# Seven down products in the first half of a SwiGLU block, with sums on preloaded PSUM banks and weight remainders split during attention

## The chip, the cores and the metric

The kernel runs on one core of a Trainium2 chip. The metric is the device time of one execution in microseconds (us); lower is better. The engines are named as in the profile: PE is TensorE (matmuls; PEld its weight loads), DVE is VectorE, ACT is ScalarE, POOL is GpSimd, SP is SyncE, which here issues DMAs.

## The reference

One transformer block over 2048 tokens of width 576, all in float32: a layer norm modulated by a condition vector, an attention with 32 heads of 18 in four segments of 512 tokens with a linear memory carried from segment to segment, then a second modulated norm and a SwiGLU feed-forward network of width 4608.

```python
h = _layernorm(x) * (1 + ca) + sa
x = x + ga * _A_ref(h, A_wq, A_wk, A_wv, A_wo, A_beta)   # attention, 4 segments, memory M, z
h = _layernorm(x) * (1 + cb) + sb
x = x + gb * ((_silu(h @ w_gate) * (h @ w_up)) @ w_down) # 576 -> 4608 -> 576
```

## The kernel before

The block runs in three stages: projections (to about 270 us), attention (to about 610 us), and the feed-forward network. Float32 matmuls are done by splitting an operand into a rounded high part (`fp32r`) and a low remainder (original minus high part), and adding three products: high x high, high x low, low x high. So each operand costs a cast on ScalarE (`wh`, `ah`, `dh`) and a subtraction on VectorE (`wl`, `al`, `dl`).

**Attention.** 32 units u (segment, group of four heads), each of 11 steps k. Per unit, TensorE makes the scores of one unit twice: once for the row maxima (L182, reduced by VectorE at L187), once shifted by the maxima (L599); ScalarE takes the exponentials into `Pt` (L602), GpSimd masks the diagonal (L606), TensorE multiplies by V (`av`, L619). Work of other kinds is put at fixed steps by the table `PAT`, or by `at(g, f)`, which runs f at step g = 11 u + k.

**Feed-forward.** Tokens are taken in two halves t of 1024, the hidden width in 18 passes p of 256 (`NPR`). Gate and up products are made with Strassen's scheme in Winograd's form: per pass and per z (0 gate, 1 up) seven products m of 2 x 2 blocks instead of eight, so a pass has 14 steps k, in the order `ZM`. A product is seven matmuls of 512 columns (`prod`, L1200): six on two blocks of 128 rows in their three split parts, and one on the 32 remaining rows of each 288-row block. For that one, tile `R[z]` (`wr`) holds the remaining rows three times over: high part, low part, high part. The weights of a pass lie in tile `O[p, z]`: slots 0, 1, 2, 3 are loaded, slots 3 to 6 end as sums (`sum_o`, GpSimd); the remaining rows are stored beside them, four times over, as a third group of 128 columns. In the first half `prep_r` casts the high parts into `R[z]` (ScalarE, L1149), `later` subtracts the low parts (VectorE, L1150), and `store_r` writes `R[z]` to memory (`rD`). In the second half `prep_r` loads `R[z]` from there, and `load_o` loads the sums that `store_o` stored.

The banks A (two), B and C take the products. ScalarE copies one product into bank B before the next is added to it (L1246), so sums of products are made in PSUM. `fin` takes Silu and gate times up, into `AC[i, j]`, the four blocks of the activation.

**Down projection.** The activation of pass p is multiplied by `w_down` during pass p + 1, chunk by chunk, between the products. `is_plain(t, p)` decides how: all of the first half, and the last two passes of the second half, are plain. A plain pass has eight chunks of 2 x 6 matmuls of 288 columns, four activation blocks (`prep_a`) and four weight blocks (`prep_d`), and each chunk is added by VectorE to its accumulator (L1325). A pass that is not plain has seven products of two chunks each, of 2 x 3 matmuls; it needs sums of activation blocks (`sum_a`, VectorE, L1271), seven `prep_a` and seven `prep_d`, and its fourteen chunks are added by VectorE to eight accumulators `acc[0..7]` (L1309), which are combined at the end (`comb`). The weights of a pass lie in the one tile `RW[p]`: loaded (`load_d`), multiplied by the output gate (`mul_d`, GpSimd), summed (`sum_d`, GpSimd), and stored for the second half (`wdD`). Plain chunks run at the steps set in `CH0[t]`, the others at those in `CH` (two at steps 4 and 11, none at 6 and 13).

All chunks use two PSUM tiles of two banks each, in turn (tag `dn`). The first half also makes the second half's operands (`prep2`: norm of the last tokens, transposes into a `dn` tile, splits on ScalarE and VectorE, sums on GpSimd, stores by SyncE), step by step in passes 1 to 16.

Every engine works through its instructions in the order in which the program lists them. The order within a step k is: weight casts for five products ahead (`prep_w`, `PF` = 5), subtractions left over from the step before (`later`), Silu that waited (`acts`), the product, loads, sums, the chunk, `prep_d`, `prep_a`.

The lines of the code that a sentence can't say are these; `POS` gives the product of chunks 2i and 2i + 1:

```python
CH = (1, 1, 1, 1, 2, 1, 0, 1, 1, 1, 1, 2, 1, 0)
ZM = [(z if m != 3 else 1 - z, m) for z in range(2) for m in (1, 3, 6, 2, 7, 5, 4)]
POS = [1, 4, 2, 5, 6, 7, 3]
```

Of the kernel before, what the change touches and what calls it, by code (L numbers as in the profile page):

```python
# [15 lines left out]
P = 128  # L16
# [21 lines left out]
CH0 = ((0, 0, 0, 0, 1, 1, 1, 1, 1, 1, 1, 1, 0, 0), (0, 0, 0, 1, 1, 1, 1, 1, 1, 1, 1, 0, 0, 0))  # L38
RS = {(0, 5): 2, (0, 6): 4, (0, 8): 3, (0, 10): 5, (1, 9): 2, (1, 11): 3, (1, 13): 4}
# [24 lines left out]
LNA = 1  # L64
S1B, S2B, XB, WB = 2, 2, 2, 1
# [7 lines left out]
def block(ctx: ExitStack, tc: tile.TileContext, x, wqk, wv, wo, beta, wgu, wd, c, w_mod, out):  # L73
# [76 lines left out]
    rD = [[dr.tile([96, 7, P], F32, tag=f"rD{p}_{z}", name=f"rD{p}_{z}") for z in range(2)] for p in range(NF // 2)]  # L150
# [898 lines left out]

    def prep2(x2p):  # L1050
# [4 lines left out]
        def opr(kb, hv, o, f):  # L1055
            n = P if kb < 2 else 96
            st = x2p.tile([P, 2, 256], F32R, tag="st", name="st", bufs=4)
# [28 lines left out]
        for kb in range(3):  # L1086
            n = P if kb < 2 else 96
            for hv in range(2):
                for kh in range(2):
# [10 lines left out]
                    pt = ps.tile([P, 2, L], F32, tag="dn", name="pt", bufs=2)[:, 0].rearrange("p (a b) -> p a b", b=P)  # L1100
# [31 lines left out]
    def load_o(t, p, z):  # L1132
        O[p, z] = o = opl.tile([P, 7, 3, P], F32, tag="O", name="O", bufs=2)
        if t == 0:
            nc.sync.dma_start(o[:, 0:4], wgu[p, z])
        else:
            nc.sync.dma_start(o[:, 0:3, 0:2], wgu[p, z][:, 0:3, 0:2])
            nc.sync.dma_start(o[:, 3:7, 0:2], oD[p][z])

    def store_o(p, z):  # L1140
        nc.scalar.dma_start(oD[p][z], O[p, z][:, 3:7, 0:2])

    def prep_r(t, p, z, part=0):
        r = R[z]
        if t == 1:
            (nc.sync if p or z == 0 else nc.scalar).dma_start(f32(r[0:96]), rD[p][z])
            return
        o, c = O[p, z], slice(0, 3) if part == 0 else slice(3, 7)
        nc.scalar.copy(r[0:96, c], o[0:96, c, 2, :])  # L1149
        later.append(lambda: nc.vector.tensor_tensor(r[32:64, c], o[32:64, c, 2, :], f32(r[32:64, c]), op=ALU.subtract))  # L1150

    def sum_o(p, z, j, eng=nc.gpsimd):
        o = O[p, z]
        d, a, b, op = ((4, 3, 2, ALU.add), (5, 4, 0, ALU.subtract), (3, 0, 3, ALU.subtract), (6, 1, 5, ALU.subtract))[j]
        eng.tensor_tensor(o[:, d], o[:, a], o[:, b], op=op)  # L1155

    def store_r(p, z):
        nc.scalar.dma_start(rD[p][z], f32(R[z][0:96]))

    def prep_w(p, z, m):  # L1160
        o = O[p, z][:, SLOT[m], 0:2]
# [123 lines left out]

    def load_x11(t):
# [9 lines left out]
    def down(t, p, c):  # L1296
        m, c = POS[c // 2], c % 2
        ah, al = AP[p % 2, m]
        dh, dl = DP[p % 2, m]
        pd = ps.tile([P, 2, L], F32, tag="dn", name="pd", bufs=2)  # L1300
        for i in range(2):
            tk = slice(128 * (2 * c + i), 128 * (2 * c + i) + 128)
            for k, (a, w) in enumerate(((ah, dh), (ah, dl), (al, dh))):
                nc.tensor.matmul(pd[:, i, :288], lhsT=a[:, tk], rhs=w, start=(k == 0), stop=(k == 2))  # L1304
        o = acc[m][:, 2 * c:2 * c + 2]
# [5 lines left out]
    def plain(t, p, c):  # L1311
        b, h, c = c // 4, c // 2 % 2, c % 2
        pd = ps.tile([P, 2, L], F32, tag="dn", name="pd", bufs=2)
# [9 lines left out]
        d = x11[1] if t and b and h else acc[2 + h + 2 * b]  # L1323
# [8 lines left out]
    def comb(j):  # L1332
        d, b = ((2, 1), (0, 5), (6, 1), (5, 6), (3, 5), (7, 6), (4, 7), (0, 7))[j]
        d = acc[d] if d else x11[1]
        nc.vector.tensor_tensor(d, d, acc[b], op=ALU.add)

    def is_plain(t, p):
        return t == 0 or p >= NPR - 2

    with tc.manual_schedule():  # L1340
# [5 lines left out]
        for u in range(NU + 1):  # L1346
# [4 lines left out]
            for k in range(11):  # L1351
                next(ga, None)
                next(gb, None)
                if u == 17 and k == 0:
# [30 lines left out]
        load_o(0, 0, 1)  # L1385
        load_y(0, 1)
# [13 lines left out]
        for i in range(4):  # L1400
            for h in range(2):
                for c in range(WC):
# [12 lines left out]
                    if n in WW:  # L1415
                        j = WW.index(n)
                        if j < 2:
                            prep_r(0, 0, 0, j)
# [26 lines left out]
        for t in range(2):  # L1445
            for p in range(NPR):
                last = t == 1 and p == NPR - 1
# [3 lines left out]
                if t == 0 and p == 1:  # L1451
                    p7.close()
                    x2p = pool(p6, "x2p")
                    g2 = prep2(x2p)
                if t == 0 and p == NPR - 1:
                    run(g2)
                    p6.close()
                    accq = pool(p4, "acq")
                    new_acc(accq, (1, 6, 7))
                if last:  # L1460
                    load_x11(1)
                chunk = 0
                for k in range(14):
# [6 lines left out]
                    for f in todo:  # L1470
                        f()
                    while acts:
# [14 lines left out]
                    if t:  # L1487
                        if k == 2 + swap:
                            prep_r(1, p, 1)
                        elif not last and k == 9:  # L1490
                            prep_r(1, nx, 0)
                    else:
                        if k in (3, 5):
                            prep_r(0, p, 1, k // 5)
                        elif tn == 0 and k in (9, 10):
                            prep_r(0, nx, 0, k - 9)
                        elif tn and k == 8:
                            prep_r(1, 0, 0)
# [16 lines left out]
                        if not dl and k in (6, 7, 8, 9) and p < NPR - 2:  # L1515
                            sum_d(p, k - 6)
# [3 lines left out]
                        elif k == 3:  # L1520
                            store_r(p, 0)
                        elif k == 8:
# [112 lines left out]
```

## Time and profile before

| | us |
|---|---|
| median of 3 runs | 1904.1 (1901.33 to 1904.87) |
| profiled execution | 1902.24 |
| its span, first to last instruction | 1900.5 |
| granted TensorE clock, mean | 0.996 |

The profile is of one execution. A busy time is the time in which an engine had at least one instruction under way; group rows add up the durations of their instructions, which can overlap a little. Waits are given as "who <- whom: us in total, times, longest". The chain of waits is followed back from the last instruction of the program: at each step to what released it.

The page's view of forty equal slices shows the three stages in GpSimd's line and in the DMA's:

```profile
PE   6999999999999899999999999999999999999999
DVE  6566358878886688898898888876888888888887
ACT  1222267768767444445454454444445454454542
POOL 5212236555556555545544545400000000000000
```

Each digit is the busy share of 47.5 us in tenths; the first half of the feed-forward network is the part in which GpSimd works after the thirteenth slice, the second half the part in which it rests.

### The profile page before, as it was taken

What the parts mean: (1) busy time and instruction counts of PE and PEld (TensorE: products, weight loads), DVE (VectorE), ACT (ScalarE), POOL (GpSimd) and SP (SyncE); (2) the same over time, 40 slices, a digit from 0 to 9 for tenths busy, and PEclk for the clock granted to TensorE, in tenths of its full rate; (3) what the DMA queues carried; (4) which work ended last, traced back from release to release, by engine and by line L of the source; (5) the groups of instructions that cost most, each with busy time, mean ns of one, the idle gap of its engine ahead of it and who ended that gap; (6) DMA issues with size and microseconds to landing.
All of it is one profiled execution on the core that took longest, in us unless ns stands there. A gap on an engine that the chain in (4) does not pass through costs nothing.

```text
span 1900.5 us, 30716 instructions
## 1 busy us (share of the span) xinstructions
PE 1862.9 (98%) x10927; PEld 1559.2 (82%) x10927; DVE 1509.0 (79%) x3277; ACT 933.8 (49%) x2060; POOL 584.4 (31%) x789
## 2 busy tenths in 40 slices
PE   6999999999999899999999999999999999999999
PEld 4888866676766788888888888888888888888888
DVE  6566358878886688898898888876888888888887
ACT  1222267768767444445454454444445454454542
POOL 5212236555556555545544545400000000000000
PEclk9999999999999899999999999999999999999999
DMA  6767555446654854454454454378343233333331
GB/s 190 259 221 249 200 193 155 132 136 175 184 159 127 282 201 160 157 196 158 153 189 158 164 171 149 135 262 257 102 123 104 85 115 102 124 102 101 108 108 59
DMA packets 179424, 304.31 MB, mean 160 GB/s; under 512 B 26152, under 2 KB 107688, under 8 KB 177352
## 3 DMA queue, kind: packets, MB, share of 16 engines
q1 hardware_dynamic: 150696, 245.29, 40.9%
q10 hardware_dynamic: 28576, 57.07, 8.6%
q8 instruction: 86, 1.41, 0.3%
q14 instruction: 66, 0.54, 0.1%
HBM read 187.98 MB, written 113.77 MB: 159 GB/s over the span
## 4 chain that ended last, share of the span: by engine, by line
PE 90%; DVE 3%; DMA 2%; ACT 2%; POOL 1%; issue 1%; SPq 0%; ACTq 0%; DVEq 0%; POOLq 0%
PE A L1200 23%; PE pd L1321 13%; PE C L1200 12%; PE pd L1304 9%; PE B L1200 6%; PE pp L99 6%; PE s L599 4%; PE av L619 4%; PE s L182 4%; PE pv L99 2%; PE pw L729 2%; PE pn L800 1%; PE px L640 1%; ACT Pt L602 1%; PE pm L448 1%
## 5 line engine op out<-in xcount | busy, mean ns | idle before, releaser
L1200 PE MATMUL A<-y,wh 128*128 128x512 f32 x1152 | 404.5, 392 | 1.7 <-ACT B L1246 1.1
L187 DVE CUSTOM_DVE_ANT_0 junk<-s,tri 128x256 bf16<-128x256 f32 (+3 forms) x512 | 228.4, 486 | 68.4 <-PE s L182 60.9
L1165 DVE TENSOR_TENSOR wl<-O,wh 128x256 fp32r<-128x256 f32 x504 | 264.1, 529 | 3.3 <-ACT wh L1164 2.8
L1200 PEld LDWEIGHTS A<-y,wh 128*128 128x128 f32 x1152 | 216.7, 188 | 42.6 <-ACT B L1246 1.7
L1200 PE MATMUL A<-y,wl 128*128 128x512 f32 x576 | 224.8, 390 | 0.0
L602 ACT ACTIVATE Pt<-s 128x512 f32<-128x512 f32 (+1 forms) x352 | 187.9, 559 | 70.2 <-PE s L599 64.4
L1155 POOL TENSOR_TENSOR O<-O 128x384 f32<-128x384 f32 x140 | 158.1, 1142 | 174.3 <-DMA O<-in_wgu_dram 78.8
L1200 PE MATMUL C<-y,wh 128*128 128x512 f32 x576 | 203.6, 394 | 3.8 <-DMA y<-yD 2.5
L1309 DVE TENSOR_TENSOR acc<-acc,pd 128x576 f32<-128x576 f32 x216 | 162.2, 751 | 54.8 <-PE pd L1304 50.6
L1164 ACT CAST wh<-O 128x256 fp32r<-128x256 f32 x504 | 196.9, 405 | 0.8 <-issue 0.7
L1321 PE MATMUL pd<-dh,ah 128*128 128x288 f32 x640 | 189.8, 297 | 0.3 <-DVE acc L1325 0.3
L1321 PE MATMUL pd<-dh,al 128*128 128x288 f32 x640 | 188.2, 294 | 0.0
L1321 PE MATMUL pd<-dl,ah 128*128 128x288 f32 x640 | 188.1, 294 | 0.0
L1325 DVE TENSOR_TENSOR acc<-acc,pd 128x576 f32<-128x576 f32 x156 | 116.7, 749 | 81.8 <-PE pd L1321 81.7
L1264 ACT CAST ah<-sg 128x512 fp32r<-128x512 f32 x192 | 119.3, 621 | 86.1 <-DVE sg L1224 80.4
L599 PE MATMUL s<-qs,ks 110*128 110x512 f32 (+2 forms) x384 | 150.1, 407 | 2.9 <-ACT Pt L602 2.4
L182 PE MATMUL s<-ks,qs 108*128 108x256 f32 (+3 forms) x512 | 140.4, 327 | 1.9 <-DVE mx L187 1.8
L1265 DVE TENSOR_TENSOR al<-sg,ah 128x512 fp32r<-128x512 f32 x192 | 135.6, 707 | 7.1 <-ACT ah L1264 6.8
L1304 PE MATMUL pd<-dh,ah 128*128 128x288 f32 x448 | 132.9, 297 | 0.0
L1304 PE MATMUL pd<-dl,ah 128*128 128x288 f32 x448 | 131.9, 294 | 0.0
L1304 PE MATMUL pd<-dh,al 128*128 128x288 f32 x448 | 131.2, 293 | 0.0
L1200 PEld LDWEIGHTS C<-y,wh 128*128 128x128 f32 x576 | 108.1, 188 | 24.1 <-DMA y<-yD 2.9
(364 smaller groups left out, 4410.9 us busy)
## 6 DMA issues: line engine op xcount, KB each, us to landing
O<-in_wgu_dram SPq DMA_DIRECT2D x36, 768.0 KB
oD<-O ACTq DMA_DIRECT2D x36, 512.0 KB
O<-oD SPq DMA_DIRECT2D x36, 512.0 KB
ks<-kD SPq DMA_DIRECT2D x64, 216.0 KB
qs<-qD SPq DMA_DIRECT2D x64, 216.0 KB
O<-in_wgu_dram SPq DMA_DIRECT2D x36, 384.0 KB
rD<-wr ACTq DMA_DIRECT2D x36, 336.0 KB
wr<-rD SPq DMA_DIRECT2D x35, 336.0 KB
```

The source lines that it names most:

```text
L99: nc.tensor.matmul(ps, lhsT=a, rhs=b, start=(k == 0), stop=(k == 13))
L182: nc.tensor.matmul(bank[:, n * (h - h0):n * (h - h0) + n], lhsT=qst[b][0:108, h, 128 * i:128 * i + 128], rhs=kst[b][0:108, h // 2, 0:n], s ...
L187: nc.vector.tensor_tensor_reduce(junk[:, :n], bank[:, n * (h - h0):n * (h - h0) + n], tri[:, L - n:], 1.0, -3e38, op0=ALU.add, op1=ALU.max ...
L599: nc.tensor.matmul(bank[:, n * (g - h):n * (g - h + w)].rearrange("p (a b) -> p a b", a=w), lhsT=kst[u % NB][0:110, g // 2, 128 * j:128 * ...
L602: nc.scalar.activation(pt[:, h:h + per, :n], bank[:, :n * per].rearrange("p (a b) -> p a b", a=per), AF.Exp, scale=SCALE)
L1155: eng.tensor_tensor(o[:, d], o[:, a], o[:, b], op=op)
L1164: nc.scalar.copy(wh, o)
L1165: later.append(lambda: nc.vector.tensor_tensor(wl, o, f32(wh), op=ALU.subtract))
L1200: nc.tensor.matmul(bank, lhsT=a, rhs=b, start=(first and n == 0), stop=(n == 6), skip_group_check=not first)
L1304: nc.tensor.matmul(pd[:, i, :288], lhsT=a[:, tk], rhs=w, start=(k == 0), stop=(k == 2))
L1309: nc.vector.tensor_tensor(o, o, pd[:, :, :288], op=ALU.add)
L1321: nc.tensor.matmul(pd[:, i, :288], lhsT=a[:, tk], rhs=w, start=(k == 0), stop=(k == 5))
```

## The change

Five edits, which need each other:

1. `is_plain` no longer holds for the first half, but for its last two passes: passes 0 to 15 of the first half are multiplied with seven products. Their accumulators `acc[1]`, `acc[6]`, `acc[7]` are set up at pass 1 instead of pass 17, `acc[5]` becomes one of the eight, and what it held is kept in `x11[0]`, loaded at pass 17; `comb` runs at the end of both halves.
2. In the first half, from the pass after pass 1 on, the first chunk of a step whose number is in `AS` is not added by VectorE: ScalarE copies the accumulator into the chunk's `dn` tile before the product of the step (`preload`), the chunk's matmuls add to it, and ScalarE copies the sum back at the start of the next step (`outs`). It is done where the same tile was last written by a chunk (`dn_ok`); after a transpose of `prep2` the chunk is added by VectorE as before. The program has 87 such preloads.
3. The split of the remaining weight rows is made in attention (`stage_r`): nine blocks, 22 steps apart; each is a load, four sums on GpSimd, four casts on ScalarE and four subtractions on GpSimd at single steps, and two stores. Four remainders lie on the 128 partitions of a block. `load_r` then loads `R[z]` in both halves, with three DMAs of 32 partitions.
4. `O` has no third group of columns any more: the sums, loads and stores of `O` are two thirds as wide, and contiguous.
5. `mul_d` moves from steps 4 and 5 to step 3, `sum_d` from steps 6 to 9 to steps 4 and 5, the first four `sum_o` from steps 4 to 7 to steps 5 to 8. `prep2` has three `st` tiles instead of four.

```diff
-CH0 = ((0, 0, 0, 0, 1, 1, 1, 1, 1, 1, 1, 1, 0, 0), (0, 0, 0, 1, 1, 1, 1, 1, 1, 1, 1, 0, 0, 0))
+CH0 = (0, 0, 0, 1, 1, 1, 1, 1, 1, 1, 1, 0, 0, 0)
+AS = (1, 3, 6, 8, 10, 13)
...
+    def stage_r():
+        big = flat(yh12.rearrange("p a b c -> p (a b) c"))
+        ts = [big[:, 896 * i:896 * i + 896].rearrange("p (a b) -> p a b", b=P) for i in range(3)]
+        for b in range(NF // 4):
+            o, h, g = ts[b % 2], ts[2].bitcast(F32R), 22 * b
+            at(max(0, g - 8), lambda b=b, o=o: nc.sync.dma_start(o[:, 0:4], wgr[b]))
+            for j, (d, x_, y_, op) in enumerate(SUMS):
+                at(g + 3 + j, lambda o=o, d=d, x_=x_, y_=y_, op=op: nc.gpsimd.tensor_tensor(o[:, d], o[:, x_], o[:, y_], op=op))
+            for j in range(4):
+                c = slice(32 * j, 32 * j + 32)
+                at(g + 11 + j, lambda o=o, h=h, c=c: nc.scalar.copy(h[:, :, c], o[:, :, c]))
+                at(g + 12 + j, lambda o=o, h=h, c=c: nc.gpsimd.tensor_tensor(o[:, :, c], o[:, :, c], f32(h[:, :, c]), op=ALU.subtract))
+
+            def save(b=b, o=o, h=h):
+                nc.sync.dma_start(rD[b][0], f32(h))
+                nc.sync.dma_start(rD[b][1], o)
+            at(g + 19, save)
...
+    def new_dn(name, ok=True):
+        dn_ok.append(ok)
+        return ps.tile([P, 2, L], F32, tag="dn", name=name, bufs=2)
...
-        O[p, z] = o = opl.tile([P, 7, 3, P], F32, tag="O", name="O", bufs=2)
+        O[p, z] = o = opl.tile([P, 7, 2, P], F32, tag="O", name="O", bufs=2)
...
+    def load_r(p, z):
+        b, g = divmod(2 * p + z, 4)
+        for i in range(3):
+            nc.sync.dma_start(f32(R[z][32 * i:32 * i + 32]), rD[b][i % 2][32 * g:32 * g + 32])
...
+    def preload(t, p, c):
+        if t == 0 and p > 0 and c in AS and dn_ok[-2]:
+            PRE[c] = pd = new_dn("pd")
+            nc.scalar.copy(pd[:, :, :288], chunk_of(c))
...
+        pd = PRE.pop(c, None)
+        add = pd is None
...
-                nc.tensor.matmul(pd[:, i, :288], lhsT=a[:, tk], rhs=w, start=(k == 0), stop=(k == 2))
+                nc.tensor.matmul(pd[:, i, :288], lhsT=a[:, tk], rhs=w, start=(add and k == 0), stop=(k == 2),
+                                 skip_group_check=not add)
+        if not add:
+            outs.append(lambda: nc.scalar.copy(o, pd[:, :, :288]))
+            return
...
     def is_plain(t, p):
-        return t == 0 or p >= NPR - 2
+        return p >= NPR - 2
...
+                    while outs:
+                        outs.pop(0)()
+                    if prev is not None and not is_plain(*prev) and CH[k]:
+                        preload(*prev, chunk)
...
-                        if k in (3, 5):
-                            prep_r(0, p, 1, k // 5)
-                        elif tn == 0 and k in (9, 10):
-                            prep_r(0, nx, 0, k - 9)
...
+                    if k == 2 + swap:
+                        load_r(p, 1)
+                    elif not last and k == 9:
+                        load_r(nx, 0)
...
-                        elif not dl and k in (4, 5):
-                            mul_d(p, k - 4)
-                        if tn == 0 and 4 <= k < 8:
-                            sum_o(nx, 0, k - 4)
+                        elif not dl and k == 3:
+                            mul_d(p, 0)
+                            mul_d(p, 1)
+                        if not dl and k in (4, 5) and p < NPR - 2:
+                            sum_d(p, 2 * k - 8)
+                            sum_d(p, 2 * k - 7)
+                        if tn == 0 and 5 <= k < 9:
+                            sum_o(nx, 0, k - 5)
...
-                        if not dl and k in (6, 7, 8, 9) and p < NPR - 2:
-                            sum_d(p, k - 6)
```

More of the change, by code (lines that the diff above doesn't have):

```diff
@@ L1322, in plain @@
                     k += 1
-        d = x11[1] if t and b and h else acc[2 + h + 2 * b]
+        d = x11[t] if b and h else acc[2 + h + 2 * b]
         o = d[:, 2 * c:2 * c + 2]
@@ L1446, in block @@
             for p in range(NPR):
-                last = t == 1 and p == NPR - 1
+                end = p == NPR - 1
+                last = t == 1 and end
                 dl = 2 if t == 0 and p == 0 else 0
```

92 lines of the change are left out of this document (40 added, 52 removed).

## The prediction

> **What bounds the kernel now.** I read the page's busy times first, then a table of stretches, then the chain of waits inside single passes, then the groups of VectorE, ScalarE and GpSimd, and last who waits for whom.
>
> ```profile
> span 1900.5 us, 30716 instructions
> PE 1862.9 (98%) x10927; PEld 1559.2 (82%) x10927; DVE 1509.0 (79%) x3277; ACT 933.8 (49%) x2060; POOL 584.4 (31%) x789
> ...
> 270.00:350.00 80.00, 78.62 (x568) 49.21 (x569) 69.40 (x290) 63.51 (x133) 48.58 (x90) 1.00 0.47 139
> 350.00:480.00 130.00, 129.94 (x962) 91.47 (x961) 105.02 (x438) 98.63 (x199) 67.23 (x132) 1.00 0.52 153
> ...
> 670.00:705.00 35.00, 32.67 (x183) 28.52 (x182) 30.12 (x50) 15.83 (x36) 18.46 (x18) 1.00 0.49 171
> 845.00:1055.00 210.00, 209.71 (x1169) 185.88 (x1168) 179.73 (x266) 101.44 (x236) 101.87 (x92) 1.00 0.50 168
> 1265.00:1300.00 35.00, 35.00 (x195) 30.98 (x194) 18.88 (x36) 11.56 (x28) 0.00 (x0) 1.00 0.97 334
> 1400.00:1600.00 200.00, 200.00 (x1087) 175.90 (x1086) 173.39 (x322) 97.78 (x227) 0.00 (x0) 1.00 0.34 107
> ```
>
> A window row gives the length, then the busy time of PE, weight loads, DVE, ACT and POOL, the granted clock, the DMA share and GB/s. The stretch 845 to 1055 is six passes of the first half, 1400 to 1600 about six of the second. In both TensorE is busy all of the time at full clock. VectorE is next: 179.73/6 = 30.0 us of a 35.0 us pass. The second half shows that a pass with fourteen chunks can run without a TensorE gap, but there GpSimd is idle; in the first half it works 17.0 us per pass.
>
> How long TensorE itself needs comes from the chain of waits (start, length, what):
>
> ```profile
> 1034.34 1.59 PE pd L1321 x12
> 1035.92 1.59 PE C L1200 x7
> ...
> 1399.92 0.80 PE pd L1304 x6
> 1400.72 1.59 PE B L1200 x7
> ```
>
> A product (seven matmuls) holds the chain 1.59 us, an old-style chunk (twelve) 1.59, a chunk of one of the seven products (six) 0.80. An old pass is 14 x 1.59 + 8 x 1.59 = 35.0 us, a new one 14 x 1.59 + 14 x 0.80 = 33.4. Both agree with the windows (14 passes take 490 us, the second half 33.4 each).
>
> **What is removed on TensorE.** Sixteen passes (those whose predecessor is pass 0 to 15 of the first half) change from 96 down matmuls to 84. That is 35.0 - 33.4 = 1.59 us each, 25.4 us in all, on the engine that sets the end. Weight loads overlap and fall with it. Everything below asks how much of it is given back.
>
> **VectorE in a first-half pass.** Rows of the first half above, of the second below (name, shapes, count, busy us, mean ns):
>
> ```profile
> L1165 DVE TENSOR_TENSOR wl<-O,wh 128x256 fp32r<-128x256 f32 x83 | 52.3, 638 | 0.0
> L1265 DVE TENSOR_TENSOR al<-sg,ah 128x512 fp32r<-128x512 f32 x24 | 17.4, 727 | 1.4 <-ACT ah L1264 1.4
> L1150 DVE TENSOR_TENSOR wr<-O,wr 32x512 fp32r<-32x512 f32 x11 | 14.5, 1320 | 0.3
> L1150 DVE TENSOR_TENSOR wr<-O,wr 32x384 fp32r<-32x384 f32 x12 | 8.7, 724 | 0.7 <-ACT wr L1149 0.3
> L1062 DVE TENSOR_TENSOR st<-ha,st 128x256 fp32r<-128x256 f32 x14 | 8.5, 610 | 0.0
> L1190 DVE TENSOR_TENSOR dl<-dr__12180,dh 128x288 fp32r<-128x288 f32 x4 | 3.7, 919 | 0.1
> L1190 DVE TENSOR_TENSOR dl<-dr__12568,dh 128x288 fp32r<-128x288 f32 x4 | 2.9, 730 | 0.1
> ...
> L1309 DVE TENSOR_TENSOR acc<-acc,pd 128x576 f32<-128x576 f32 x83 | 62.4, 751 | 21.8 <-PE pd L1304 20.2
> L1165 DVE TENSOR_TENSOR wl<-O,wh 128x256 fp32r<-128x256 f32 x83 | 34.7, 418 | 0.0
> L1265 DVE TENSOR_TENSOR al<-sg,ah 128x512 fp32r<-128x512 f32 x42 | 28.7, 683 | 0.0
> L1271 DVE TENSOR_TENSOR sg<-sg 128x512 f32<-128x512 f32 x24 | 16.4, 683 | 0.0
> L1190 DVE TENSOR_TENSOR dl<-dr__18649,dh 128x288 fp32r<-128x288 f32 x7 | 3.2, 451 | 0.0
> ```
>
> Start from a second-half pass: 173.39/200 x 33.4 = 29.0 us. Six of the fourteen evictions go to ScalarE (the program has 87 preloads, so nearly six in each of fifteen passes): -6 x 0.75. The preparation of the second half's operands stays, about three splits at 0.42 without company (as wl): +1.3. That leaves 25.7 us if GpSimd did not exist. The two halves differ by GpSimd: wl is 0.638 instead of 0.418, dl about 0.82 (mean of the two rows) instead of 0.451, st 0.610 instead of wl's 0.418, and two wr splits of 1.320 and two of 0.724 would be about 0.68 and 0.55 by al and wl. Per pass that is 14 x 0.22 + 4 x 0.37 + 3 x 0.19 + 1.6 for wr, and about 0.4 for the rest: 7.1 us lost to 17.0 us of GpSimd, 0.42 for each.
>
> GpSimd's own rows (first half):
>
> ```profile
> L1155 POOL TENSOR_TENSOR O<-O 128x384 f32<-128x384 f32 x46 | 52.8, 1161 | 61.7 <-DMA O<-in_wgu_dram 39.4 <-DVE sg L1215 12.1 <-DVE wl L1165 9.9
> L1108 POOL TENSOR_TENSOR t<-ha 128x256 f32<-128x256 f32 x3 | 2.4, 802 | 0.5 <-ACT ha L1104 0.5
> ```
>
> The eight weight sums shrink from 384 to 256 columns, 1.16 to 0.80 us: GpSimd falls to 14.1 us per pass. The low end for VectorE is 25.7 + 0.42 x 14.1 = 31.6 us. The high end charges every operation as if GpSimd had not become shorter: 14 x 0.22, seven dl and the four sums of sg that Strassen's products need at 0.37, 1.2 for the others (al, st, sg), which gives 34.1. TensorE needs 33.4. The middle, 32.9, is nearly level with it, so VectorE changes from an engine with 5 us to spare to one with almost none, and its late moments will reach TensorE. I take 0.5 us of stall per pass (0 to 1.2), 7.5 us over fifteen passes. Pass 1 has no preloads (its predecessor is pass 0), so all fourteen evictions are VectorE's, +4.5 us of load; 670 to 705 shows that the early passes already leave TensorE idle 2.3 us. I take 2 us (0 to 4).
>
> The skill's rule speaks against the change here: the Trainium skill, SBUF — State Buffer, section Who interferes with whom, says that a VectorE instruction with two SBUF inputs and a GpSimd instruction reading SBUF exclude each other for the whole instruction. The trace agrees: wl (two SBUF inputs) takes 638 against 418 ns beside GpSimd. All ten operations that the change adds per pass are of this kind, all six that it hands to ScalarE (one input in PSUM) are not; by it the sum would use the high end, and the time would be the second rival's.
>
> **ScalarE and the preload.** Copies between SBUF and a PSUM bank of 576 columns have no row; the nearest:
>
> ```profile
> L1164 ACT CAST wh<-O 128x256 fp32r<-128x256 f32 x82 | 31.5, 404 | 0.0
> L1264 ACT CAST ah<-sg 128x512 fp32r<-128x512 f32 x23 | 14.3, 621 | 21.6 <-DVE sg L1224 21.6
> L1246 ACT COPY B<-A 128x512 f32<-128x512 f32 x12 | 6.9, 572 | 9.6 <-PE A L1200 9.6
> L1149 ACT CAST wr<-O 96x512 fp32r<-96x512 f32 x12 | 7.4, 620 | 0.0
> L761 ACT ACTIVATE xh<-xr,nb,rs 128x576 f32<-128x576 f32 x5 | 4.3, 868 | 1.0 <-POOL nb L760 1.0
> ```
>
> Between 0.57 (fewer columns) and 0.87 (the same, with scale and bias) I take 0.65. ScalarE: 101.44/6 = 16.9 us, minus 2.2 for the wr casts (two at 0.62, two of three quarters that size), plus 3 x 0.62 (ah), 3 x 0.43 (dh, between wh and ah), 12 x 0.65: 25.7 of 33.4 us. It has room, but a preload waits for the bank, TensorE's chunk waits for the preload, and behind the preload stand the Silu, the copy out of bank A and the next casts. Where the bank was last used by a preloaded chunk it is read back a step earlier, and nothing waits. At chunks 6 and 13 it was evicted by VectorE: from the end of chunk 4 to the start of 6 lie one chunk and one product, 0.80 + 1.59 = 2.39 us, of which eviction and preload take 0.75 + 0.65. So VectorE may be about 0.9 us late there. It is later than that today:
>
> ```profile
> 1040.70 1.59 PE pd L1321 x12
> ...
> 1044.40 0.74 DVE L1325 TENSOR_TENSOR acc<-acc,pd 128x576 f32<-128x576 f32 x1
> ...
> PEld pd L1321 <- DVE acc L1325: 0.9, 2, 0.7
> ```
>
> The chunk ended at 1042.29, its eviction began at 1044.40, 2.1 us late; with an old-style chunk's longer spacing that cost nothing (TensorE waited for VectorE 0.9 us in all the first half). That happened while GpSimd worked without a break. The moves of its multiplications and subtractions to steps 3 to 5 put that stretch on chunks 4 and 5, and the end of a stall shifts chunk 5's eviction next. This is part of the 0.5 us.
>
> **Attention.** Nine blocks of remainders, from step 0 to about step 195 of 363, in the first 20 of 32 units:
>
> ```profile
> L809 ACT COPY nm<-pn 128x380 f32<-128x380 f32 (+1 forms) x16 | 7.1, 442 | 5.9 <-PE pn L800 5.9
> L205 ACT COPY mr<-pmt 32x128 f32<-32x128 f32 x20 | 4.8, 240 | 0.0
> L815 POOL TENSOR_TENSOR nm<-nm 128x76 f32<-128x76 f32 x8 | 2.8, 348 | 0.1
> ...
> PEld s L599 <- ACT Pt L602: 12.8, 21, 1.0
> ```
>
> 36 copies on ScalarE of 224 columns lie between 0.24 and 0.44, taken as 0.35: 12.6 us. 36 sums (128 columns) and 36 subtractions (224) on GpSimd, between 0.35 and 0.80: about 0.48 and 0.72, 43 us. From 350 on TensorE is busy 129.94 of 130 us and ScalarE 76%, so the later twenty copies hide. In 270 to 350 TensorE waited 12.8 us for ScalarE's exponentials; sixteen copies there are 5.6 us, of which I charge 3. GpSimd rises from about half to three quarters; it masks the diagonal of Pt two steps or more before TensorE needs it: 1 us. Together 4 us, bounds 0 and 14 (all copies, and a little of GpSimd). A gain is excluded, since what was dropped here (the first block's splits) lay beside TensorE.
>
> **Costed at nothing.** SyncE: 27 more issues in attention and three wr loads of 32 partitions in place of one store or load. A wr load has five steps (12 us) before its first use; ahead of it in the queue stand waits for VectorE:
>
> ```profile
> SPq L1063 <- DVE st L1062: 52.8, 9, 8.3
> ```
>
> At most 8.3, so it holds; were it late, products would start late by the rest. The eight combining adds at the end of the first half (1152 columns, twice 0.683) are 11 us on VectorE, which has 18.88 of 35 there and no GpSimd beside it. The contiguous O tile and fewer bytes change no wait of TensorE.
>
> **Sum.** Against the profiled execution, 1902.24 us (span 1900.5): 1902.2 - 25.4 + 7.5 + 2 + 4 = 1890. The runs shown have a median of 1904.1, 1.9 higher, and reach down to 1901.33; I leave 1890.
>
> **Rivals.** (1) All is hidden: VectorE at its low end, attention 2 us: 1902.2 - 25.4 + 2 = 1879. For it the regular second half, against it the missing spare time. (2) VectorE is the bound: its high end of 34.1 us plus the 0.5 us of late moments makes a pass 34.6, 15 x 1.2 = 18 is given back, and with 2 + 4 the time is 1901, up to 1906 if pass 1 and attention cost their worst. For it the 638 against 418. That is the skill's rule, SBUF — State Buffer, at work. (3) Slower: the preload at chunks 6 and 13 meets the lateness seen, 2.1 + 0.75 + 0.65 = 3.5 against 2.39, and TensorE stands 1.1 us twice per pass, 33 us: 1902.2 - 25.4 + 33 + 6 = 1916. It decides from (25.4 - 6)/30 = 0.65 us per place, a lateness of about 1.6 us. Against it: the moved GpSimd work is shorter, and a stalled TensorE lets VectorE catch up. (4) Attention pays its 14 us in full: 1890 + 10 = 1900; against it the saturated TensorE from 350 on.
>
> **Chances and range.** Forecast 0.48, (1) 0.17, (2) 0.15, (3) 0.13, (4) 0.07. What can be told from no change is about 0.2%, 3.8 us: faster means below 1900.3, slower above 1907.9. Faster: 0.48 + 0.17 + about a third of (2) and half of (4) = 0.74. Slower: (3), 0.13. The same: the rest, 0.13. The range runs from (1) to the upper end of (2), 1879 to 1906; it leaves out (3) and a little below (1). The forecast's own range is 1883 to 1898.
>
> **What would show it.** Right: down matmuls of the 288 kind fall by 192, first-half passes last 33.4 to 34.5 us, VectorE is busy over 94% in them, and TensorE's few gaps there end on VectorE's evictions or ScalarE's preloads. Wrong: first-half passes of 35 us or more; preloads of chunks 6 and 13 that begin over 1.6 us after the end of chunks 4 and 11; units of attention longer by over 0.5 us after 350; waits of products for wr.

## The result, and the profile after

| | before | after |
|---|---|---|
| median, us | 1904.2 | 1926.4 (4 runs, 1923.9 to 1928.7) |
| ratio | | 1.0123, 95% interval 1.0108 to 1.0139 |
| profiled execution, us | 1902.24 | 1928.66 |

The change makes the kernel slower by 22 us; 1890 was forecast. The page's busy times and the same stretches as before, moved where a stage moved:

```profile
span 1926.9 us, 31120 instructions
PE 1855.3 (96%) x10735; PEld 1538.7 (80%) x10735; DVE 1542.4 (80%) x3382; ACT 1052.4 (55%) x2294; POOL 594.6 (31%) x861
...
270.00:350.00 80.00, 76.71 (x528) 48.00 (x528) 66.42 (x270) 62.79 (x138) 60.41 (x114) 0.96 0.61 188
350.00:480.00 130.00, 125.67 (x930) 87.89 (x932) 102.18 (x422) 98.13 (x208) 84.68 (x165) 1.00 0.60 184
675.00:710.00 35.00, 33.66 (x182) 29.20 (x181) 34.79 (x63) 16.19 (x39) 15.03 (x16) 1.00 0.53 180
845.00:1055.00 210.00, 199.27 (x1061) 172.25 (x1060) 183.23 (x290) 139.56 (x302) 90.47 (x88) 0.98 0.47 153
1285.00:1320.00 35.00, 27.98 (x140) 23.48 (x140) 14.57 (x28) 9.95 (x22) 0.00 (x0) 0.96 0.99 307
1400.00:1600.00 200.00, 200.00 (x1086) 175.77 (x1085) 173.42 (x322) 97.17 (x225) 0.00 (x0) 1.00 0.35 108
```

The 192 matmuls are gone (10927 to 10735), and the second half still runs without a gap. But in 845 to 1055 TensorE, full before, now stands for 10.7 us; around 1300 it has gaps too, and so it has in attention (125.67 of 130 us busy in 350 to 480, where it had been full). VectorE, which was to be the tight engine, is busy 183.23 of 210 us there, 87%: it has time to spare, and TensorE waits all the same.

Where the time went is read from one marker, ScalarE's copy of bank A into B, which comes twice a pass. The rows give duration (min, median, max), then the first and last start, here over passes 1 to 17 and over the first pass of the second half; before, then after:

```profile
L1246 ACT COPY B<-A x35: 570/570/582, 673.9 to 1275.9; 128x512 f32<-128x512 f32 x35
L1246 ACT COPY B<-A x3: 570/570/570, 1275.9 to 1311.1; 128x512 f32<-128x512 f32 x3
```

```profile
L1265 ACT COPY B<-A x35: 570/570/581, 675.5 to 1293.1; 128x512 f32<-128x512 f32 x35
L1265 ACT COPY B<-A x3: 570/570/570, 1293.1 to 1337.2; 128x512 f32<-128x512 f32 x3
```

All that lies ahead of pass 1 costs 1.6 us more (675.5 against 673.9). Of all the parts this is the least certain: in four experiments below whose programs are the same up to there (the first, second, fourth and sixth), the marker comes at 669.7, 670.5, 669.8 and 675.3. Passes 1 to 17 went from 602.0 to 617.6, +15.6, where -15.9 was forecast (-25.4 + 7.5 + 2). The pass at the border of the halves went from 35.2 to 44.1, +8.9, where nothing was forecast. Together 26.1 of the 26.4 us between the spans of these two executions; the medians are 22 us apart.

**The first half.** Waits in the first half of after (who, for whom, us, times, longest); neither was there before:

```profile
ACT pd L1314 <- DVE acc L1346: 40.6, 16, 4.1
PE pd L1338 <- ACT pd L1314: 22.5, 14, 2.6
```

The expectations below speak of 54.8 us: they add the 32.3 us that weight loads (PEld) waited for the same preloads, which overlap the 22.5.

One such wait, first in the timelines of TensorE and VectorE (the first row is the first matmul of chunk 5, so chunk 4 is done), then in the chain of waits:

```profile
903.79 0.29 PE L1338 MATMUL pd<-dh,ah 128*128 128x288 f32 x1
```

```profile
902.95 1.03 DVE L1088 TENSOR_TENSOR st<-ha,st 128x256 fp32r<-128x256 f32 x1
903.90 1.03 DVE L1184 TENSOR_TENSOR wl<-O,wh 128x256 fp32r<-128x256 f32 x1
904.85 1.22 DVE L1284 TENSOR_TENSOR al<-sg,ah 128x512 fp32r<-128x512 f32 x1
905.99 1.21 DVE L1290 TENSOR_TENSOR sg<-sg 128x512 f32<-128x512 f32 x1
...
909.98 0.68 DVE L1290 TENSOR_TENSOR sg<-sg 128x512 f32<-128x512 f32 x1
910.58 0.41 DVE L1088 TENSOR_TENSOR st<-ha,st 128x256 fp32r<-128x256 f32 x1
```

```profile
907.13 0.75 DVE acc L1346
...
907.90 0.65 ACT pd L1314
...
908.60 1.06 PE pd L1338 x6
```

Chunk 4 is done at 903.8, but VectorE adds it only at 907.13, because st, wl, al and a sum of sg stand ahead of it on VectorE, each slow (a sum takes 1.21 us here and 0.68 at 909.98, st 1.03 and then 0.41). Chunk 6 uses chunk 4's tile: its preload follows at 907.90 and its matmuls at 908.60, while the product before it had ended at about 906.3. That is the prediction's place, chunk 6, with a lateness of 3.3 us where 0.9 is free. Why is VectorE slow just here? GpSimd's timeline:

```profile
896.77 3.49 POOL L1197 TENSOR_TENSOR dr__11720<-dr__11720,gbB 128x576 f32<-128x576 f32 x2 [9.07 <-DVE cu L1242]
900.22 4.42 POOL L1202 TENSOR_TENSOR dr__11720<-dr__11720 128x288 f32<-128x288 f32 x4
...
907.75 1.42 POOL L1177 TENSOR_TENSOR O<-O 128x256 f32<-128x256 f32 x2
```

It works for 12.4 us without a break (896.77 to 909.17), from the multiplications that edit 5 moved to step 3 to the weight sums. VectorE's four sums of activation blocks stand at steps 2 to 5, three of them inside this stretch here. Their group in the first half, then in the second, where GpSimd rests:

```profile
L1290 DVE TENSOR_TENSOR sg<-sg 128x512 f32<-128x512 f32 x64 | 74.1, 1158 | 0.0
...
L1290 DVE TENSOR_TENSOR sg<-sg 128x512 f32<-128x512 f32 x39 | 26.7, 684 | 0.0
```

1158 ns against 684. The rule that the prediction cited (the Trainium skill, SBUF — State Buffer, section Who interferes with whom) names this kind, two inputs in SBUF beside a GpSimd that reads SBUF, and the trace agrees.

**The clock.** A stall can cost more than its length. The same place in the next pass, in the chain, and two stretches with their granted clock (third number from the end of a row):

```profile
944.90 1.49 PE pd L1338 x6
946.38 2.75 PE A L1219 x7
```

```profile
945.00:947.00 2.00, 2.00 (x8) 1.84 (x9) 2.00 (x5) 1.23 (x3) 0.00 (x0) 0.58 0.00 0
947.00:949.00 2.00, 2.00 (x7) 1.48 (x6) 0.64 (x2) 0.65 (x2) 0.00 (x0) 0.57 0.00 0
```

After a gap of some 2.5 us TensorE runs at about half clock for 3.4 us: the chunk takes 1.49 instead of 0.80, the product 2.75 instead of 1.59. In the stretches of 2 us this shows at four places of the first half (727, 799, 947, 1021), 4 us at 0.58, so about 1.7 us lost each. The length of the gap does not decide it: in PE's timeline seven gaps in passes 1 to 17 last 2.0 us or more, and the half clock follows those that end at 726.2 (2.3 us), 797.7 (2.0), 944.9 (2.5) and 1020.4 (2.5), but not those at 908.6 (2.3), 983.8 (2.55) and 1093.6 (2.3). The Trainium skill, TensorE: Matmul & The Clock Gate, section What's actually happening, has the clock halved after an idle window of about 3.4 us that runs freely; here gaps of 2.0 to 2.5 us were enough, at four places of seven.

**The border.** The chain there and what TensorE waited for:

```profile
1297.01 10.80 DMA y<-yD
...
1307.83 9.89 DMA wr<-rD
...
1317.76 0.80 PE A L1219
...
PE A L1219 <- DMA wr<-rD: 5.4, 2, 5.0
```

Before, up's remainders of this pass came over ScalarE's queue; now `load_r` puts them on SyncE behind the loads of the activations, whose tile is freed only as the last pass ends.

**Attention.** The copies of `av` after the change, then before, and the chain in the unit that grew most:

```profile
L633 ACT COPY avs<-av x32: 561/587/591, 268.0 to 624.6; 128x512 f32<-128x512 f32 x32
```

```profile
L631 ACT COPY avs<-av x32: 572/587/590, 268.8 to 614.9; 128x512 f32<-128x512 f32 x32
```

```profile
290.88 6.08 DMA qs<-mr
...
297.10 0.77 PE s L601
```

Attention takes 356.6 us instead of 346.1, +10.5 in these two executions; in the seven experiments below that leave it as it is, the same copies span 352.8 to 356.1 us. The cost lies in the units in which remainder blocks are made: up to the 21st copy (491.6 before, 501.3 after) all 10.5 us are lost, and from there to the last copy both kernels take 123.3 us. One cause can be seen in the unit shown, where row maxima (`mr`) are queued behind SyncE's new loads. From the last of these copies to the first marker 59.0 became 50.9 us (47.9 to 52.6 in those seven experiments); the first block's casts, splits and wide weight sums are gone there. That gives back 8.1.

### The profile page after: what moved, and what is told of

It is laid out like the page before. It is cut to its first block, busy times and chain, and to the rows that moved or that the text cites. A ratio compares the mean times of both kernels' runs of the same rounds, so it can differ in the third digit from the quotient of the medians.

```text
span 1926.9 us, 31120 instructions
## 1 busy us (share of the span) xinstructions
PE 1855.3 (96%) x10735; PEld 1538.7 (80%) x10735; DVE 1542.4 (80%) x3382; ACT 1052.4 (55%) x2294; POOL 594.6 (31%) x861
## 4 chain that ended last, share of the span: by engine, by line
PE 76%; DVE 12%; DMA 4%; ACT 3%; issue 3%; POOL 2%; SPq 0%; ACTq 0%; DVEq 0%; POOLq 0%
PE A L1219 20%; PE pd L1338 15%; PE C L1219 9%; PE pp L101 5%; PE B L1219 4%; PE s L601 4%; PE av L621 3%; PE s L184 3%; PE pv L101 3%; DVE wl L1184 2%; PE pd L1358 2%; DVE sg L1290 2%; DVE acc L1346 2%; PE pw L731 2%; DVE al L1284 1%
## 5 line engine op out<-in xcount | busy, mean ns | idle before, releaser
L1338 PE MATMUL pd<-dh,ah 128*128 128x288 f32 x896 | 269.0, 300 | 24.0 <-ACT pd L1314 22.5
L1338 PE MATMUL pd<-dl,ah 128*128 128x288 f32 x896 | 264.5, 295 | 0.0
L1338 PE MATMUL pd<-dh,al 128*128 128x288 f32 x896 | 263.4, 294 | 0.0
L1338 PEld LDWEIGHTS pd<-dh,ah 128*128 128x128 f32 x896 | 168.8, 188 | 49.6 <-ACT pd L1314 32.3
L1338 PEld LDWEIGHTS pd<-dl,ah 128*128 128x128 f32 x896 | 170.0, 190 | 14.9
L1284 DVE TENSOR_TENSOR al<-sg,ah 128x512 fp32r<-128x512 f32 x240 | 171.2, 713 | 5.5 <-ACT ah L1283 5.3
L1338 PEld LDWEIGHTS pd<-dh,al 128*128 128x128 f32 x896 | 169.7, 189 | 0.0
L1177 POOL TENSOR_TENSOR O<-O 128x256 f32<-128x256 f32 x140 | 121.3, 883 | 147.7 <-DMA O<-in_wgu_dram 71.4
L1283 ACT CAST ah<-sg 128x512 fp32r<-128x512 f32 x240 | 149.0, 621 | 28.3 <-DVE sg L1243 24.3
L1219 PEld LDWEIGHTS C<-y,wh 128*128 128x128 f32 x576 | 108.9, 189 | 24.1 <-DMA y<-yD 4.4
L1219 PEld LDWEIGHTS A<-y,wl 128*128 128x128 f32 x576 | 109.3, 190 | 15.3
```

Source lines behind the costliest of these rows:

```text
L1219: nc.tensor.matmul(bank, lhsT=a, rhs=b, start=(first and n == 0), stop=(n == 6), skip_group_check=not first)
L1283: nc.scalar.copy(ah, src)
L1284: later.append(lambda: nc.vector.tensor_tensor(al, src, f32(ah), op=ALU.subtract))
```

## The experiments

The theory: in the first half, edit 5 holds GpSimd on VectorE's sums just before chunk 4 is added, and chunk 6's preload passes the delay on to TensorE; the border and attention are separate losses. The main rival: VectorE has too much to do in a pass, wherever GpSimd's work stands, so the six chunks, not the moved steps, decide. Each kernel is the changed one with the edit named. Ratios are against the kernel before, run beside each (its medians lie between 1902.7 and 1904.3 us); "less" is against the changed kernel's 1926.4 us.

**Border: up's remainders back on ScalarE's queue.**

```diff
-                        load_r(p, 1)
+                        load_r(p, 1, nc.scalar if swap else nc.sync)
```

> One edit to the changed kernel: the load of the second wr tile in the first pass of the second half is issued by ScalarE's queue, as before the change, instead of SyncE's, where it stands behind fourteen loads of y. Theory (the queue it was moved to costs the 8.9 us by which the interval between passes 17 and 18 grew, 44.1 against 35.2 us): that interval falls to about 35.5 us and the time by 8 to 9 us, to about 1918 against the changed kernel's 1926.4. Rival (the y loads and stores fill the DMA engines, and wr is late in any queue): the interval stays over 42 us, the time within 2 us.

1921.9 us, ratio 1.0105 (1.0081 to 1.013). The border pass fell from 44.1 to 38.6 us, and no product waits for `wr` there; the last wait is now one for the activations (`y<-yD`, 11.4 us from issue to landing). About 5 of the 8.9 us are the queue, a little over half of what was expected; the rest stays.

**Chunk 6 added by VectorE.**

```diff
-AS = (1, 3, 6, 8, 10, 13)
+AS = (1, 3, 8, 10, 13)
```

> One edit to the changed kernel: chunk 6 is no longer preloaded by ScalarE but added by VectorE. Theory (TensorE stands at chunk 6 because VectorE evicts chunk 4 late; the preload only adds its 0.65 us behind that): the stall at chunk 6 falls from about 2 us by 0.7 us in each of fifteen passes, VectorE gets 0.75 us more, so the time changes by -10 to +5 us. Rival (the preload on ScalarE is the cause): the waits at chunk 6 vanish, -20 us or more.

1914.2 us, 1.0066 (1.005 to 1.0082): 12 us less, though VectorE has 0.75 us more per pass; at most 10 had been expected. The waits move rather than vanish:

```profile
PE pd L1338 <- DVE acc L1346: 15.2, 11, 2.2
PE pd L1338 <- ACT pd L1314: 3.4, 5, 1.3
```

VectorE is still late, now for the tile itself; what ends is the preload that stood behind it.

**No GpSimd work on `w_down`.** Passes 1 to 17 leave out `mul_d`, and passes 1 to 15 `sum_d`: the down weights are not multiplied by the output gate, and raw weights are loaded in place of their sums, so the result is another, with two more loads per pass (0.44 MB).

```diff
-                        elif not dl and k == 3:
-                            mul_d(p, 0)
-                            mul_d(p, 1)
-                        if not dl and k in (4, 5) and p < NPR - 2:
-                            sum_d(p, 2 * k - 8)
-                            sum_d(p, 2 * k - 7)
```

> The changed kernel without GpSimd's two multiplications and four subtractions on the down weights in passes 1 to 17 of the first half; the three summed slots are loaded from memory instead, so the down weights used are not scaled by the output gate and not summed. About 7 us of GpSimd per pass are gone, all of it at steps 3 to 5. Theory (VectorE's operations with two SBUF inputs wait for those GpSimd operations, so chunk 4's eviction is late): the sums of sg and the wl, al splits at steps 3 to 5 fall from about 1.2 us to 0.68 and 0.42, the waits of TensorE for preloads fall from 54.8 us to under 10, first-half passes take 33.6 to 34.3 us, and the time falls by 30 to 45 us, to 1882 to 1896. Rival (VectorE simply has too many instructions): under 12 us.

1889.0 us, 0.9927 (0.991 to 0.9944), 37 us less. The six passes again:

```profile
845.00:1055.00 210.00, 209.91 (x1145) 183.64 (x1144) 170.92 (x315) 151.79 (x329) 48.55 (x59) 1.00 0.55 175
```

TensorE is full again at full clock, with all 87 preloads in place; the sums of sg take 723 ns, and passes 1 to 17 last 580.4 us (674.0 to 1254.4). So seven products and ScalarE's sums are affordable; GpSimd's company is what costs.

**No preloads at all.**

```diff
-AS = (1, 3, 6, 8, 10, 13)
+AS = ()
```

> One edit to the changed kernel: no chunk is preloaded; VectorE adds all fourteen. VectorE gets 6 x 0.69 = 4.1 us more per pass, ScalarE loses 7.7. Theory (VectorE is the scarce engine in the first half, level with TensorE): passes grow by 1 to 3 us, the time by 15 to 45 us. Rival (preloads cost more than they relieve): the time falls.

1919.1 us, 1.0089 (1.0074 to 1.0104): 7 us less than with them, so the expectation fell. With all fourteen chunks VectorE is nearly at its limit (202.75 of 210 us), its sums are as slow as ever (1259 ns), and yet that is better than six preloads behind a late VectorE:

```profile
845.00:1055.00 210.00, 200.66 (x1082) 173.81 (x1081) 202.75 (x331) 105.31 (x244) 92.76 (x91) 1.00 0.46 149
...
PE pd L1338 <- DVE acc L1346: 12.3, 13, 1.6
PE pd L1338 <- ACT ah L1283: 11.5, 13, 1.7
```

**Edit 5 undone.** `mul_d` at steps 4 and 5, `sum_d` at 6 to 9, the first `sum_o` at 4 to 7, as before the change; all else stays.

```diff
-                        elif not dl and k == 3:
-                            mul_d(p, 0)
-                            mul_d(p, 1)
+                        elif not dl and k in (4, 5):
+                            mul_d(p, k - 4)
```

> The changed kernel with GpSimd's multiplications, subtractions and the first four weight sums back at their old steps (4 and 5, 6 to 9, 4 to 7): one multiplication alone, then weight sums in between. Theory (GpSimd's unbroken stretch on steps 3 to 5 makes chunk 4's eviction late): the stretch is broken up and moves behind chunk 6; TensorE's waits for preloads fall from 54.8 us to 15 to 35, the time by 8 to 25 us from 1926.4. Rival (GpSimd's amount decides, wherever it lies): within 4 us.

1901.3 us, 0.9986 (0.9974 to 0.9997), 25 us less. VectorE's sums are fast again, though GpSimd does the same work:

```profile
L1290 DVE TENSOR_TENSOR sg<-sg 128x512 f32<-128x512 f32 x64 | 46.4, 725 | 0.0
...
845.00:1055.00 210.00, 208.52 (x1133) 181.55 (x1132) 187.42 (x312) 150.24 (x326) 91.43 (x95) 1.00 0.50 159
```

725 against 1158 ns, in the same tiles and number, and passes 1 to 17 last 591.5 us (674.3 to 1265.8) instead of 617.6: the whole gain lies there, at the upper end of what was expected. GpSimd still has a long stretch without a break in the pass shown above (895.21 to 905.09, 9.9 us), but now it starts as chunk 4 ends, behind three of the four sums. So its place is what counts. This is the theory's step, shown by itself; the rival, for which only amounts count, had no place for it.

**Chunks 4, 5 and 6 at steps 4, 5 and 6** instead of 4, 4 and 5, in the first half.

```diff
+CHA = (1, 1, 1, 1, 1, 1, 1, 1, 1, 1, 1, 2, 1, 0)
...
+                        for _ in range((CH if prev[0] else CHA)[k]):
```

> One edit to the changed kernel: in the first half the chunks 4, 5 and 6 run at steps 4, 5 and 6, one each, instead of two at step 4, one at 5 and none at 6. From the end of chunk 4 to the start of 6 lie then two products and a chunk, 3.98 us instead of 2.39. Theory (the lateness is 1.5 to 3.5 us, and 0.99 us of it fits now, 2.58 us then): the stall at chunk 6 falls from about 2 us to 0 to 0.8 us, the time falls by 15 to 28 us, to 1898 to 1911. Rival (VectorE is over its time in a pass, and a stall spared here comes up at a later chunk): less than 8 us, with waits at chunks 8 to 13.

1909.4 us, 1.0032 (1.002 to 1.0044), 17 less. More room between chunk 4's end and chunk 6 brings two thirds of what undoing edit 5 brings, with GpSimd's steps left as they are and the sums still at 1140 ns; the mechanism can be cut at either end.

**Attention: the remainder blocks loaded one step later, stored three steps earlier.**

```diff
-            at(max(0, g - 8), lambda b=b, o=o: nc.sync.dma_start(o[:, 0:4], wgr[b]))
+            at(max(0, g - 7), lambda b=b, o=o: nc.sync.dma_start(o[:, 0:4], wgr[b]))
...
-            at(g + 19, save)
+            at(g + 16, save)
```

> Two steps moved in the changed kernel's attention: a block's load one step later, just behind the small loads of the score maxima instead of just ahead, and its two stores three steps earlier, so that ten steps instead of seven lie between them and the next maxima. Theory (those small loads wait for the block's DMAs; unit 2 took 13.8 instead of 9.9 us with 6.1 us on that load): attention, 10 us longer than before, gets 4 to 7 us shorter; the whole time falls by 0 to 6 us, as the start of the feed-forward part took 8 us of the 10 back. Rival (the added work of ScalarE and GpSimd makes attention longer): attention within 2 us.

1922.4 us, 1.0098 (1.0076 to 1.012). In the profiled run the copies of `av` run from 272.3 to 624.3, 352.0 us instead of 356.6; in the median it is 4 us, within the scatter of both. But the first experiment, with attention untouched, has 352.8 us, so this one pair shows little. Over all profiles, five with the two steps moved (this one and the last four) span 351.7 to 352.9 us, eight without 352.8 to 356.6: some 2.5 us on average, a quarter of attention's loss and less than the 4 to 7 expected. The rest is open (GpSimd's and ScalarE's new work was not taken out by itself).

**The first half plain again**: edits 1, 2 and 5 undone; remainders in attention, the narrow `O` and `load_r` stay.

```diff
-        return p >= NPR - 2
+        return t == 0 or p >= NPR - 2
```

> The changed kernel with seven products, preloads and moved steps undone: the first half is plain as before, only the remainders made in attention, the narrower weight tile and the three-part wr loads stay. Theory (these edits cost 10 us in attention, give 8 back at the start, and lose 9 at the border of the halves): first-half passes 35.0 to 35.3 us, the border's interval 40 to 45 us, the time 1906 to 1912. Rival (they gain by themselves, since VectorE loses 4 us of wr splits per pass): 1890 to 1900.

1909.1 us, 1.0028 (1.0017 to 1.004): edits 3 and 4 cost some 6 us net. Its passes 1 to 17 last 602.1 us (667.6 to 1269.7; the profiled execution, 1904.15 us, is the fastest of ten), as before the change: the splits taken off VectorE and the narrower sums gain nothing where TensorE is full.

**Four mends together**: the old steps, the remainder load on ScalarE's queue, attention's moved loads and stores, and the store of `w_down` at step 8 in the first half's last pass.

```diff
-                        if k == 12 + dl // 2:
+                        if k == (8 if end else 12 + dl // 2):
```

> The changed kernel with four edits at once: the GpSimd steps put back as before, the remainder load of the border on ScalarE's queue, the attention's loads and stores moved as in the run before the last, and, new, the store of the w_down matrices in the first half's last pass at step 8 in place of 12, so that no load of the activations at the border waits for it. Theory (the three places are separate and their gains add): the 1901.3 of the steps alone, less 4 to 5 for the load, less 4 for attention, less 1 to 3 for the earlier store: 1889 to 1893. Rival (what one place gives is waited for at the next, because the same queues and VectorE carry it): 1896 to 1901, the same as the steps alone.

1894.3 us, 0.9945 (0.9932 to 0.9958): 7 us better than the steps alone, just outside the theory's range. The new edit gave nothing that can be seen: the border pass is 39.3 us (1265.8 to 1305.1), against 38.6 with the queue alone.

**The same with chunk 10 left to VectorE.**

```diff
-AS = (1, 3, 6, 8, 10, 13)
+AS = (1, 3, 6, 8, 13)
```

> The run before with chunk 10 taken from the six chunks that ScalarE preloads and adds, so VectorE adds nine in place of eight. With the GpSimd steps back, the largest single gaps left on PE stand before chunk 10's product, where the preload is late by 0.4 to 1.7 us in 11 of the passes. Theory (the preload of this chunk is late, and VectorE has the time): 5 to 10 us under the run before. Rival (VectorE is the limit again, as its share of a pass would grow by 0.9 us): 3 to 10 us over it.

1886.6 us, 0.9907 (0.9893 to 0.9922), faster than both kernels, 17.8 us under the one before measured beside it.

```profile
845.00:1055.00 210.00, 209.59 (x1142) 183.23 (x1141) 198.15 (x318) 144.34 (x316) 94.91 (x96) 1.00 0.50 158
...
PE pd L1338 <- ACT pd L1314: 1.2, 3, 0.6
```

TensorE waits 1.2 us for preloads instead of the changed kernel's 22.5. Over passes 1 to 17 VectorE is busy 556.5 us here and 556.7 in the changed kernel, but the passes take 585.8 us instead of 617.6. It is not VectorE's load that decides but when its instructions come.

**The same with chunks 4, 5 and 6 spread** (chunk 10 preloaded again).

> The run before the last with chunks 4, 5 and 6 spread over steps 4, 5 and 6 in the first half. Theory (spreading helped only because the GpSimd steps crowded VectorE at step 4; with those gone nothing is left for it): within 3 us of the run with the four edits. Rival (the spread has a gain of its own, since the preload of chunk 6 has a step more): 4 to 10 us under it.

1894.6 us, 0.9958 (0.994 to 0.9976), 0.3 from the run with the four mends: once GpSimd stands elsewhere, spreading has nothing to mend.

**Gate's remainder load of the border on ScalarE's queue too** (to the version without chunk 10).

```diff
-                        load_r(nx, 0)
+                        load_r(nx, 0, nc.scalar if end else nc.sync)
```

> The run with four edits and without chunk 10 once more, with the other remainder load of the border too (gate's, before the products of the second half begin) on ScalarE's queue. In that run the border interval is still 38.0 us, against 35.2 before the change, the wait that ends it is one for the activations' load, and SyncE, which issues those loads, itself waits 8.1 us for the three remainder loads that stand ahead of them. Theory (these waits hold the activations back): the border interval falls to 35 to 36 us, the time by 2 to 4 us, to 1882.5 to 1884.5. Rival (the DMA engines are full at the border, a share of 1.00 and over for 30 us, and nothing that only reorders the loads helps): 1886 to 1888.

1887.5 us, 0.9911 (0.9894 to 0.9927): no gain, the border pass 38.8 us (1256.8 to 1295.6). The time is the rival's, and reordering does not help. But full DMA engines are not the whole answer: in the kernel before, too, their share was 1.02 from 1265 to 1285, and TensorE had no gap there. Why the border was 35.2 with the same activations to load stays open.

## Why the prediction was wrong

**Right.** TensorE's saving, nearly: 192 matmuls fewer, and with GpSimd's work on `w_down` left out, where TensorE is full, passes 1 to 17 are 21.6 us shorter than before, where 25.4 was forecast. In the version without chunk 10 they fall to 585.8 us (669.5 to 1255.3), 16.2 under before where 15.9 was forecast; that is another kernel, with the late moments mended and five preloads, so the agreement is partly luck. The preload's 0.65 us, and the way back, in the first half:

```profile
L1314 ACT COPY pd<-acc 128x576 f32<-128x576 f32 x87 | 56.0, 644 | 40.6 <-DVE acc L1346 40.6
L1341 ACT COPY acc<-pd 128x576 f32<-128x576 f32 x87 | 55.8, 641 | 44.8 <-PE pd L1338 44.3
```

Pass 1's early gaps did not grow: TensorE is busy 33.66 of 35 us there against 32.67 before. ScalarE's load held too, 139.56/210 x 36.3 = 24.1 us a pass against 25.7. The combining adds at the border are on no chain.

**The step that failed.** "I take 0.5 us of stall per pass": the stall was priced from VectorE's total, found level with TensorE, with the late moments a small part of it. The total came out at 183.23/210 x 36.3 = 31.7 us, at the prediction's low end, and the stall came all the same. Of the 41 us given back in passes 1 to 17 (25.4 + 15.6), TensorE stood idle for 27.0 (1.2 before; 22.5 are waits for preloads) and lost some 7 to the halved clock: about 2.2 us of stall per pass where 0.5 was taken. The other 8 are in neither; some 4 of them are the smaller saving, and the rest stays open. Rival 3 named the mechanism and, in "the moves of its multiplications and subtractions to steps 3 to 5 put that stretch on chunks 4 and 5", its cause. It was given 0.13, and two reasons against it, and both failed: the moved work is shorter in sum, but it stands unbroken where three of VectorE's four sums are; and VectorE does catch up while TensorE is stalled, but only after the damage, and the next pass brings the same order. Rival 3's price was near (33 us; the forecast's 7.5 and the 31.5 by which passes 1 to 17 missed it make 39), but its places were not: it had 1.1 us at chunks 6 and 13, and in PE's timeline it is 1.4 to 2.6 us at chunk 6, in ten passes, and nothing at chunk 13, with the half clock on top. Rival 2 names the kind of instruction that is slowed, but prices it as a total; its sum has a slip as well, since pass 1 and attention at their worst (4 and 14 us) make 1901 + 2 + 10 = 1913, not 1906. The signs that the prediction gave for being wrong all came: passes of 36.3 us, a preload of chunk 6 that begins 4.1 us after the end of chunk 4, longer units of attention after 350, and products waiting for `wr` at the border.

**"Costed at nothing".** The remainder load was checked against its distance in a usual pass (five steps, 12 us) and against SyncE's waits there, not at the border, where the loads of the activations stand ahead on the same queue. The pass there grew by 8.9 us, about 5 of them by the queue. The change removes the line that had kept this load on ScalarE's queue.

**Attention** was priced at 4 net and came to 1.6 in these executions, from two sizes that were both missed: +10.5 where it had 4, and 8.1 given back at the start of the network, which the prediction had put beside TensorE and so at nothing. The step that failed in the first is "the later twenty copies hide": between 350 and 480 TensorE, busy 129.94 of 130 us before, is busy 125.67. The second was a gain held to be excluded. In the chain of before that work was on the path:

```profile
628.50 1.03 POOL O L1155
...
631.62 0.63 ACT wr L1149
...
632.27 0.68 DVE wr L1150
```

## What to carry to other kernels

Where a bank must be filled before a product can add to it, the price is the slack of that one chain (the last eviction, the copy, the matmul), read at the step where it stands; an engine's total says little about it. When a change moves work of GpSimd, lay its new stretch over VectorE's instructions with two SBUF inputs and see what is queued behind them. When a load changes its queue, look at the one pass in which that queue is full, not at the usual one.

## What the hardware showed that was not expected

What GpSimd's company costs VectorE depends on its place: the same 64 sums took 1158 ns in the changed kernel and 725 with edit 5 undone, with GpSimd's work about the same in the six passes (90.47 and 91.43 us). A stall of 2.0 to 2.5 us can halve TensorE's clock for 3.4 us (0.58 and 0.57 in the two stretches after 945), and one as long need not (1.00 after the 2.55 us that end at 983.8): four of the seven in passes 1 to 17 did. A copy of 128x576 between SBUF and PSUM takes ScalarE the same in both directions, 644 and 641 ns.
